# k and v of linear attention fetched as 112 rows and 16 more, in place of 115 and one

## The chip, the cores and the metric

The kernel runs on one core of one Trainium2 chip. The metric is the device time in microseconds; 926.72 us is the median of three runs of the kernel before (926.64 to 927.29). Times inside the kernel are taken from one profiled execution, whose span is 926.5 us. In the profile the engines are PE (TensorE, matrix products), DVE (VectorE), ACT (ScalarE), POOL (GpSimd) and SP (SyncE, which here does nothing but issue transfers). "SPq" is SP's queue: its rows are the times that SP spends on issuing a transfer, not the transfer itself.

## The reference

Linear attention without a softmax, an RMS norm, and a two-layer network with the activation h * erf(softplus(h)):

```python
# q, k, v: (8 batches, 8 heads, 576 positions, 64), float32
kv  = einsum('bhsd,bhse->bhde', k, v)          # 64 x 64 for each head
out = einsum('bhsd,bhde->bhse', q, kv)
out = out / sqrt(mean(out * out, axis=-1) + 1e-6) * g_norm
x   = out.transpose(0, 2, 1, 3).reshape(4608, 512)
h   = x @ w_in                                  # 512 -> 2048
g   = h * erf(softplus(h))
y   = g @ w_out                                 # 2048 -> 512, float32
```

What the change concerns is the first line: kv is a sum over the 576 positions, so it doesn't matter which position lies in which row of which chunk, as long as k and v agree.

## The kernel before

**Stages.** The 4608 tokens are worked in nine token tiles of 512: for each of the eight batches its first 512 positions, and a ninth tile with the last 64 positions of all batches (`x_last`). The network has 16 slices of 128 hidden columns. Tiles 0 and 1 are worked slice by slice in the loop at L822 (step `n` = 0 to 32). Meanwhile `w_in` and `w_out`, which come as 64-bit floats, are turned into float32 (`load_w`, `w_split`, `w_join`, L208 to L263), and from tile 1 on they are cut into three forms [...] and are stored in device memory (`w_upper`, `w_lower`, L645 to L674). From tile 2 on the loop at L976 (step `m`) works four slices at a time: each step reads four `w_in` and four `w_out` pieces of 768 KB back (`load_parts`, L765, issue at L773). A product is a group of eight matmuls into `n_ps` and four into `m_ps` (`product`, L626).

**Attention beside it.** Two heads make a pair, so a batch has four pairs. While tile T is in the network, the four pairs of batch T+1 go through attention, one in each step `m`. `visit` (L428) multiplies q with the kv of the present pair and then forms the kv of the next pair (`kv_products`, L320): five chunks of rows, and for each chunk, each half of its rows and each head one 64-column product at L449, 20 in all. Rows 0 to 63 are the first half, the rest the second. The first pair of batch 1 is done the same way by `prepare` (L353, matmuls at L357). Batch 0 goes another way (`products`, L398): six chunks of 96 rows, fetched in the first microseconds.

**The fetches.** `load_pair` (L123) fetches k and v of one pair. For batches 1 to 7 the 576 positions are cut into five chunks, 576 = 5 * 115 + 1: a first transfer (L141) brings 115 rows of 2 heads x 5 positions x 64 numbers, in which a row holds five successive positions (1280 bytes from one place of device memory), and a second (L146) brings position 575 into row 115 of chunk 0, for both heads. `load_q` (L152) then brings q of the pair in eight pieces (L162), two for each quarter of the partitions, with runs of 32 numbers (128 bytes). `turn` (L314) transposes q in 32 x 32 blocks on DVE (L318) for the visit.

**What sets the order.** The program is written out by hand (`tc.manual_schedule()`, L103): each engine does its instructions in the order of the source. All transfers named here, from the fifth pair on, go out on SP's queue one after another; an issue whose buffer is still in use holds up all behind it. `k_sb`, `v_sb` and `q_sb` have two buffers each (`kvp`), the `w_in` pieces four (`w_in_p`), and the `w_out` pieces seven (`w_out_p`). In the loop at L976 the pieces of weights are asked for at the places given by `FETCH`, one or two at a time, and the pair's loads are part of an attention piece (`loads`, L552):

```python
FETCH = ("", "in", "in", "out", "in", "out", "in", "out out")
places = (0, 2, 3, 5, 6, 8)
```

Of the kernel before, what the change touches and what calls it, by code (L numbers as in the profile page):

```python
# [61 lines left out]
def kernel(  # L62
# [12 lines left out]
    B, H, S, D = q.shape  # L75
# [43 lines left out]
    def chunks(T):  # L119

        return 6 if T == 0 else 5

    def load_pair(i, turned=True):  # L123
        T, p = divmod(i, NP)
        if T >= B:
            return
        pool = early if i in (2, 3) else kvp
        side = nc.scalar if i < 3 else nc.sync
        if T == 0:
            t = pool.tile([P, G if pool is early else S], FP32, name="q_sb", tag="q")  # L130
            t = q_sb[T, p] = t[:, 0:G].rearrange("p (j h d) -> p j h d", j=J, h=2)
            nc.sync.dma_start(
                out=t, in_=q[T, 2 * p : 2 * p + 2, 0:G, :].rearrange("h (p j) d -> p j h d", j=J)
            )
        for name, got, src in (("k", k_sb, k), ("v", v_sb, v)):
            C = chunks(T)
            rows, rest = divmod(S, C)
            assert rest < 2
            t = got[T, p] = pool.tile([rows + rest, 2, C, D], FP32, name=f"{name}_sb", tag=name)
            heads = src[T, 2 * p : 2 * p + 2]  # L140
            side.dma_start(  # L141
                out=t[:rows].rearrange("r h c d -> r h (c d)"),
                in_=heads[:, : S - rest].rearrange("h (r c) d -> r h (c d)", c=C),
            )
            if rest:
                side.dma_start(  # L146
                    out=t[rows:, :, 0], in_=heads[:, S - rest :].rearrange("h r d -> r h d")
                )
        if T > 0 and turned:
            load_q(i)  # L150

    def load_q(i):  # L152


        T, p = divmod(i, NP)
        t = q_sb[T, p] = kvp.tile([P, S], FP32, name="q_sb", tag="q")
        for n in range(P // SQ):
            h, w = divmod(n, D // SQ)
            to = t[n * SQ : n * SQ + SQ].rearrange("a (j b) -> a j b", b=SQ)
            for head, js in ((1 - h, slice(0, G // 2 // SQ)), (h, slice(G // 2 // SQ, S // SQ))):  # L160
                src = q[T, 2 * p + head, :, w * SQ : w * SQ + SQ]
                nc.sync.dma_start(  # L162
                    out=to[:, js], in_=src.rearrange("(j a) b -> a j b", a=SQ)[:, js]
                )
# [12 lines left out]
    for i in range(NP - 1):  # L177
        load_pair(i)
        if i == 0:
            load_last(0)  # L180
            load_last(1)
# [138 lines left out]
    def kv_products(T, p, at, crossed):  # L320


        ks, vs = (x.pop((T, p)) for x in (k_sb, v_sb))
        C = chunks(T)
        for c in range(C):
            for r in range(2):
                rows = (slice(0, D), slice(D, S // C + (c < S % C)))[r]
                for i in range(2):
                    yield partial(
                        nc.tensor.matmul,  # L330
                        at[rows_of[i], 1 - (r ^ i) if crossed else r, kv_cols],
                        lhsT=ks[rows, i, c],
                        rhs=vs[rows, i, c],
                        start=(c == 0),
                        stop=(c == C - 1),
                    )
# [16 lines left out]
    def prepare(T, p):  # L353

        at = at_tile()
        for product_ in kv_products(T, p, at, crossed=False):
            product_()  # L357
        kept.append(partial(kv_kept, T, p, at))
# [7 lines left out]
    def attention(T, p, pools=None, in_parts=False):  # L366
# [15 lines left out]
        def bank(name):  # L382
            if T == B:
                if p == 0:
                    at_pool(2)
                return ps_now[0].tile([P, G], FP32, name=name, tag="at")
            pool, tag = pools.get(name, (ps_at, "at"))
            return pool.tile([P, G], FP32, name=name, tag=tag)

        def square_tile(name):  # L390

            if T == 0:
                return gate.tile([P, G], FP32, name=name, tag="h")
            if apart:
                return attp.tile([P, G], FP32, name=name, tag="sq_lo")
            return qt_tile(name)[:, 0:G]

        def products():  # L398

            kv_ps = st["kv"] = bank("kv_ps")  # L400
            ks, vs, qs = (x.pop((T, p)) for x in (k_sb, v_sb, q_sb))
            C = chunks(T)
            for c in range(C):
                rows = slice(0, S // C + (c < S % C))
                for i in range(2):
                    s = rows_of[i]
                    nc.tensor.matmul(
                        kv_ps[s, s],
                        lhsT=ks[rows, i, c],
                        rhs=vs[rows, i, c],  # L410
                        start=(c == 0),
                        stop=(c == C - 1),
                    )
            if p % 2 == 0:
                nc.tensor.transpose(kv_ps[:, q_tail], q_last[:, p // 2], ident)
            st["qT"] = square_tile("qT")
            for s in rows_of:
                nc.vector.tensor_copy(out=bd[s, s], in_=kv_ps[s, s])
            if p % 2 == 0:
                tails[T] = attp.tile([P, G], FP32, name="qT_last", tag="sq_lo")[:, 0:P]  # L420
                nc.vector.tensor_copy(out=tails[T], in_=kv_ps[:, q_tail])
            st["tail"] = tails[T][:, p % 2 * R : p % 2 * R + R]
            qt_ps = bank("qt_ps")
            for j in range(J):
                nc.tensor.transpose(qt_ps[:, j * P : j * P + P], qs[:, j], ident)
            nc.scalar.copy(st["qT"], qt_ps)

        def visit():  # L428


            qT = ready.pop((T, p))
            at = st["at"] = at_tile()
            x = halves_of(qT[:, 0:G])
            for a, i in ((0, 0), (0, 1), (1, 0), (1, 1)):
                nc.tensor.matmul(  # L435
                    at[rows_of[i if a else 1 - i], a, 0 : 2 * P],
                    lhsT=bd[rows_of[i], (1 - a) * D : (2 - a) * D],
                    rhs=x[rows_of[i], a],
                    start=True,
                    stop=True,  # L440
                )
            for s in rows_of:
                nc.tensor.matmul(
                    at[s, 1, 2 * P : 2 * P + R], lhsT=bd[s, 0:D], rhs=qT[s, G:S], start=True, stop=True
                )
            st["o"] = at[:, :, 0 : 2 * P]
            if then[0] < B:
                for product_ in kv_products(*then, at, crossed=True):
                    product_()  # L449
            if apart:  # L450
                st["sq"] = x_new.tile([P, G], FP32, name="sq", tag="x")
            else:
                st["sq"] = qT[:, 0:G]
            nc.scalar.activation(two(st["sq"]), st["o"], AF.Square)
# [97 lines left out]
        def loads():  # L552
            load_pair(T * NP + p + 2)

        if T == 0:
            return products, apply, halve, mean, norm
# [174 lines left out]
    load_last(2)  # L731
    load_last(3)
    load_pair(NP - 1)

    w_rounds = {
# [86 lines left out]
    for n in range(FIRST * FC + 1):  # L822
        T, f = divmod(n, FC)
# [152 lines left out]
    for m in range(first_batch, batches + 1):  # L976
        T, b = divmod(m, NB)
# [133 lines left out]
```

## Time and profile before

| | before |
|---|---|
| median of three runs | 926.72 us |
| span of the profiled execution | 926.5 us |
| PE busy | 898.8 us |
| PE loading weights | 668.6 us |
| DVE busy | 751.0 us |
| ACT busy | 589.9 us |
| bytes moved | 259.91 MB, mean 281 GB/s |
| transfers k_sb and v_sb, first part | 56 of 287.5 KB |
| transfers k_sb and v_sb, second part | 56 of 0.5 KB |
| transfers of q_sb by L162 | 112 of 40.0 KB and 112 of 32.0 KB |
| transfers of weight pieces | 116 and 112 of 768.0 KB |
| granted TensorE clock | 1.00 throughout |

How to read the views. A group line gives the source line, the engine and the tiles, then counts and times. A wait line reads "engine tile line <- what it waited for: us in total, times, longest". A line of the chain of waits gives the start, the length and the work. A window line gives the stretch in us, its length, the busy time of each engine with the number of instructions in brackets, and at the end the clock, the share in which the core's 16 DMA engines were busy (a mean over the 16, so five busy engines alone show as 5/16 = 0.31) and GB/s. The share can show a little over 1. An engine that is busy all the time can only be made shorter by taking work from it; idle time of another engine costs nothing unless the busy one waits for it.

### The profile page before, as it was taken

The numbers are of one execution on the slowest core, as the hardware profiler recorded it, in microseconds if no ns is written. First come the engines' busy times: TensorE is split into PE (matmuls) and PEld (weight loads), VectorE is DVE, ScalarE is ACT, GpSimd is POOL, SyncE is SP. The second block draws the span as 40 slices with busy tenths as digits, with TensorE's granted clock in tenths as the row PEclk, the third lists the DMA queues.
The fourth block names the chain that finished last, engine by engine and source line by source line (L and its number), as shares of the span: only waits on it lengthen the run. The fifth ranks groups of instructions, "written<-read, shape, count | busy, mean of one in ns | idle before, by whom it ended". The sixth has DMA issues, their size and how long they took to land.

```text
span 926.5 us, 13591 instructions
## 1 busy us (share of the span) xinstructions
PE 898.8 (97%) x4990; PEld 668.6 (72%) x4990; DVE 751.0 (81%) x1088; ACT 589.9 (64%) x783; POOL 2.4 (0%) x10
## 2 busy tenths in 40 slices
PE   6999999988999999999999999999999999999998
PEld 4444445655587888778878888788878888888886
DVE  2799958888588888888888888888888888886777
ACT  3868766767675666656665666666666766665552
POOL 1000000000000000000000000000000000000000
PEclk9999999999999999999999999999999999999999
DMA  9767506698688888988898788887889788778871
GB/s 250 237 190 265 167 1 249 246 378 313 239 287 312 311 312 310 347 308 308 308 337 309 296 310 310 301 306 284 292 313 404 272 286 322 291 288 314 325 271 51
DMA packets 143210, 259.91 MB, mean 281 GB/s; under 512 B 78936, under 2 KB 101800, under 8 KB 143144
## 3 DMA queue, kind: packets, MB, share of 16 engines
q1 hardware_dynamic: 141432, 256.74, 75.7%
q10 hardware_dynamic: 1648, 2.29, 0.9%
q8 instruction: 40, 0.66, 0.3%
q14 instruction: 26, 0.21, 0.1%
q0 software_dynamic: 64, 0.00, 0.0%
HBM read 224.40 MB, written 34.60 MB: 280 GB/s over the span
## 4 chain that ended last, share of the span: by engine, by line
PE 76%; DMA 11%; DVE 6%; ACT 5%; issue 1%; SPq 1%; DVEq 0%; ACTq 0%
PE n_ps L634 41%; PE m_ps L634 20%; PE o_ps L690 6%; PE h_ps L874 4%; DMA w_out_parts<-w_out 4%; DMA w_in_parts<-w_in 2%; DMA w_in<-w_new 2%; DMA v_sb<-in_v_dram 1%; PE at_ps L449 1%; PE at_ps L435 1%; DMA w_raw<-in_moe_w_out_dram 1%; ACT s_sb L911 1%; DMA q_sb<-in_q_dram 1%; DVE h L612 1%; PE at_ps L496 1%
## 5 line engine op out<-in xcount | busy, mean ns | idle before, releaser
L634 PE MATMUL n_ps<-w_out_parts,g_forms 128*128 128x512 f32 x928 | 231.2, 391 | 1.7 <-DMA w_out_parts<-w_out 1.7
L634 PE MATMUL n_ps<-x_forms,w_in_parts 128*128 128x512 f32 x896 | 225.1, 393 | 3.2 <-DMA w_in_parts<-w_in 2.1
L634 PEld LDWEIGHTS n_ps<-w_out_parts,g_forms 128*128 128x128 f32 x928 | 172.4, 188 | 38.4 <-DMA w_out_parts<-w_out 3.3
L634 PEld LDWEIGHTS n_ps<-x_forms,w_in_parts 128*128 128x128 f32 x896 | 166.1, 188 | 41.1 <-ACT h L1024 3.2
L1039 ACT ACTIVATE s<-h 128x512 f32<-128x512 f32 x112 | 71.0, 634 | 180.9 <-DVE h L612 180.9
L612 DVE TENSOR_TENSOR h<-m_ps,h 128x512 f32<-128x512 f32 x116 | 79.9, 689 | 61.5 <-ACT h L1024 39.9
L634 PE MATMUL m_ps<-w_out_parts,g_forms 128*128 128x512 f32 (+1 forms) x468 | 124.3, 388 | 0.0
L634 PE MATMUL m_ps<-x_forms,w_in_parts 128*128 128x512 f32 x448 | 119.8, 389 | 0.0
L690 PE MATMUL o_ps<-w_out_sb,h_sb 128*128 128x512 f32 x224 | 101.5, 596 | 0.2 <-DVE h_sb L820 0.2
L634 PEld LDWEIGHTS m_ps<-w_out_parts,g_forms 128*128 128x128 f32 x468 | 87.5, 188 | 18.4
L634 PEld LDWEIGHTS m_ps<-x_forms,w_in_parts 128*128 128x128 f32 x448 | 84.1, 188 | 17.6
L612 DVE TENSOR_TENSOR e<-m_ps,e 128x512 f32<-128x512 f32 (+1 forms) x117 | 80.3, 687 | 14.1 <-PE m_ps L634 2.9
L1024 ACT ACTIVATE h<-n_ps 128x512 f32<-128x512 f32 x112 | 65.6, 585 | 16.6 <-PE n_ps L634 16.6
L690 PEld LDWEIGHTS o_ps<-w_out_sb,h_sb 128*128 128x128 f32 x224 | 41.3, 189 | 45.3 <-issue 42.8
L578 DVE SCALAR_TENSOR_TENSOR g_forms<-g_forms 128x1024 fp32r<-128x1024 f32 x58 | 71.1, 1225 | 2.0
L575 DVE TENSOR_TENSOR g_forms<-h,g_forms 128x1024 fp32r<-128x1024 f32 x58 | 70.6, 1217 | 1.2 <-ACT g_forms L572 1.1
L572 ACT ACTIVATE g_forms<-h 128x1024 fp32r<-128x1024 f32 x58 | 58.7, 1051 | 14.8 <-PE m_ps L634 10.9
L1071 DVE TENSOR_TENSOR h<-h,s 128x1024 f32<-128x1024 f32 x56 | 65.9, 1218 | 0.0
L874 PE MATMUL h_ps<-xT,w_in_sb 128*128 128x512 f32 x144 | 64.6, 594 | 0.0
L607 DVE SCALAR_TENSOR_TENSOR e<-n_ps,e 128x512 f32<-128x512 f32 x88 | 60.1, 683 | 1.5 <-PE n_ps L634 1.5
L109 ACT ACT_TABLE_LOAD x44 | 56.5, 1283 | 0.8
L874 PEld LDWEIGHTS h_ps<-xT,w_in_sb 128*128 128x128 f32 x144 | 27.1, 190 | 33.4 <-issue 31.6
(119 smaller groups left out, 990.7 us busy)
## 6 DMA issues: line engine op xcount, KB each, us to landing
w_out_parts<-w_out SPq DMA_DIRECT2D x116, 768.0 KB
w_in_parts<-w_in SPq DMA_DIRECT2D x112, 768.0 KB
w_in<-w_new SPq DMA_DIRECT2D x16, 768.0 KB
w_raw<-in_moe_w_in_dram SPq DMA_DIRECT2D x16, 512.0 KB
w_raw<-in_moe_w_out_dram SPq DMA_DIRECT2D x8, 1024.0 KB
out_dram<-e SPq DMA_DIRECT2D x32, 256.0 KB
k_sb<-in_k_dram SPq DMA_DIRECT2D x28, 287.5 KB
v_sb<-in_v_dram SPq DMA_DIRECT2D x28, 287.5 KB
```

The source lines that it names most:

```text
L109: nc.scalar.preload_act_table_set("softplus")
L572: nc.scalar.activation(high, x, AF.Copy, scale=1.0 + 2.0**-13)
L575: nc.vector.tensor_tensor(out=low, in0=x, in1=high.bitcast(FP32), op=ALU.subtract)
L578: nc.vector.scalar_tensor_tensor(out=both, in0=low.bitcast(FP32), scalar=SHIFT, in1=high.bitcast(FP32), op0=ALU.mult, op1=ALU.add,)
L607: nc.vector.scalar_tensor_tensor(out=out_, in0=ps, scalar=scale, in1=out_, op0=ALU.mult, op1=ALU.add)
L612: nc.vector.tensor_tensor(out=out_, in0=ps, in1=out_, op=ALU.add)
L634: nc.tensor.matmul(ps[:, cols], lhsT=weights(form, k), rhs=moving(form, k)[:, cols], start=(form == forms[0] and k == 0), stop=(form == fo ...
L690: nc.tensor.matmul(o_ps[j], lhsT=g[:, j * P : j * P + P], rhs=w_out_sb[:, f, :], start=(f == 0), stop=last,)
L874: nc.tensor.matmul(plain[i], lhsT=w_in_sb[:, i % FC, c], rhs=xT[T][:, c, :], start=(c == 0), stop=(c == KC - 1),)
L1024: nc.scalar.activation(h[:, i], n_ps, AF.Copy, scale=SHIFT - 1.0)
L1039: nc.scalar.activation(s[:, i], h[:, i], AF.Softplus)
L1071: nc.vector.tensor_tensor(out=part(h, half), in0=part(h, half), in1=part(s, half), op=ALU.mult)
```

## The change

The rows of the first transfer are rounded down to a multiple of 16, and what is left goes into the second transfer: 576 = 5 * 112 + 16. A new helper gives the number of rows of a chunk: 128 in chunk 0 and 112 in chunks 1 to 4 (before: 116 and 115). So the first transfer has 112 rows of 1280 bytes per head, and the second 16 rows of 256 bytes per head, into rows 112 to 127 of chunk 0. The second half of the rows in a product is 64 deep for chunk 0 and 48 for the others, in place of 52 and 51. For batch 0 (six chunks of 96) both forms give the same. The purpose is a number of rows that splits evenly over the DMA engines.

```diff
+    def rows_in(T, c):
+
+        rows = S // chunks(T) // 16 * 16
+        return rows + (S - chunks(T) * rows if c == 0 else 0)
+
     def load_pair(i, turned=True):
@@
         for name, got, src in (("k", k_sb, k), ("v", v_sb, v)):
             C = chunks(T)
-            rows, rest = divmod(S, C)
-            assert rest < 2
+            rows, rest = rows_in(T, 1), rows_in(T, 0) - rows_in(T, 1)
             t = got[T, p] = pool.tile([rows + rest, 2, C, D], FP32, name=f"{name}_sb", tag=name)
@@
-                rows = (slice(0, D), slice(D, S // C + (c < S % C)))[r]
+                rows = (slice(0, D), slice(D, rows_in(T, c)))[r]
@@
-                rows = slice(0, S // C + (c < S % C))
+                rows = slice(0, S // C)
```

The last hunk is in `products`, which serves batch 0 only. The lines after the helper are counted by five more in the changed kernel up to `load_pair`, and by four more below it: L141 becomes L145, L146 becomes L150, L162 becomes L166, L773 becomes L777.

## The prediction

> **What bounds the kernel now.** I read the page first (engine shares, slices, transfers), then the matrix engine's waits, the chain of waits, the windows, and the queue of the engine that issues the transfers.
>
> ```profile
> PE 898.8 (97%) x4990; PEld 668.6 (72%) x4990; DVE 751.0 (81%) x1088; ACT 589.9 (64%) x783; POOL 2.4 (0%) x10
> DMA  9767506698688888988898788887889788778871
> k_sb<-in_k_dram SPq DMA_DIRECT2D x28, 287.5 KB
> k_sb<-in_k_dram SPq DMA_DIRECT2D x28, 0.5 KB
> ```
>
> TensorE (PE) is busy 97%: whatever this change does, it can only take from the 926.5 - 898.8 = 27.7 us in which PE stands still. The transfers are 0.8 to 0.9 busy in most slices, a mean over 16 DMA engines. The waits of PE say which of its idle time belongs to transfers:
>
> ```profile
> PE n_ps L634 <- ACT h_sb L889: 3.4, 1, 3.4
> PE n_ps L634 <- ACT h L889: 2.8, 1, 2.8
> PE n_ps L634 <- DMA w_in_parts<-w_in: 2.1, 2, 1.7
> PE at_ps L435 <- DVE qT L318: 2.0, 1, 2.0
> PE n_ps L634 <- DMA w_out_parts<-w_out: 1.7, 2, 0.9
> ```
>
> Four waits for weights make 3.8 us in all. The 2.0 us at L435 ends with a DVE transpose of q, and that DVE instruction had itself waited 3.9 us for a q load. (7.2 us more, at L407, are the first loads of the program, which have 96 rows and don't change.)
>
> The windows show what a 115-row load does to the DMA engines. From 16.5 to 25.6 us four of them are issued (k and v of the two first pairs of batch 1):
>
> ```profile
> 21.00:22.00 1.00, 1.00 (x14) 0.93 (x11) 0.45 (x2) 0.94 (x3) 0.00 (x0) 1.00 0.98 341
> 22.00:23.00 1.00, 0.88 (x2) 0.05 (x1) 0.83 (x2) 1.00 (x3) 0.00 (x0) 1.00 0.36 132
> 24.00:25.00 1.00, 1.00 (x5) 0.60 (x4) 1.00 (x2) 1.00 (x2) 0.00 (x0) 1.00 0.34 124
> 26.00:27.00 1.00, 0.20 (x1) 0.00 (x0) 1.00 (x3) 1.00 (x3) 0.00 (x0) 1.00 0.38 133
> ```
>
> The last two columns are the DMA share and GB/s. A share of 0.34 of 16 is 5.4 engines: about five work, eleven stand idle for 5 us, at 124/5 = 24.8 GB/s each. In saturated windows (573 to 575 us: share 1.03, 420 GB/s) all 16 give 26 GB/s each.
>
> The issuing queue (SP) shows the second effect. Columns are start, length, source line:
>
> ```profile
> 573.13 0.29 SPq L141 DMA_DIRECT2D k_sb<-in_k_dram  x1
> 574.90 1.65 SPq L146 DMA_DIRECT2D k_sb<-in_k_dram  x1
> 576.59 0.42 SPq L141 DMA_DIRECT2D v_sb<-in_v_dram  x1
> 577.36 4.48 SPq L146 DMA_DIRECT2D v_sb<-in_v_dram  x1
> 581.89 7.43 SPq L162 DMA_DIRECT2D q_sb<-in_q_dram  x8
> 589.37 0.46 SPq L773 DMA_DIRECT2D w_out_parts<-w_out  x1
> 590.87 0.75 SPq L773 DMA_DIRECT2D w_in_parts<-w_in  x1
> ```
>
> Issuing two rows and eight small q pieces takes SP 16 us, and behind them four weight loads go out in a burst with nothing to wait for: they were late. SP's own waits name the cause: L162 waited 38.6 us in total on v_sb transfers and 16.7 on k_sb. The burst's fourth load is the one PE then lacks:
>
> ```profile
> 590.87 10.12 DMA w_in_parts<-w_in
> ```
>
> It lands at 601.0 and PE starts at 601.13 after 1.70 us of idleness.
>
> **What the Trainium skill says.** "DMA: Bandwidth & Descriptors", section "Why a DMA increments its semaphore by 16 and not by 1": a load from this queue uses the largest number of engines, up to 16, that divides the slowest dimension of both sides. For 115 that is 5 and for the single row (slowest dimension: 2 heads) 2; for 112 and for 16 it is 16. The trace agrees for 115 (5.4 engines); for 112 nothing here shows it, but 96-row and 128-row loads do reach share 1. Same page, "Queues, rings and completion order": every DMA engine takes the queue's pieces in order, so later loads wait behind the slow five. Same page, "Specifications": pieces under 512 B don't reach line rate; q's pieces of 128 B agree (70 to 150 GB/s at share 0.4 to 0.5 in 583 to 589 us).
>
> **The change part by part.** The instruction orders of PE, DVE, ACT and GpSimd stay as they are, and SP issues the same 651 rows with 112x2x320 in place of 115x2x320 and 16x2x64 in place of 1x2x64.
>
> Matmuls: batches 1 to 7 keep 20 products per pair; the second half of the rows is 64 or 48 deep in place of 52 or 51. In the trace 64-, 52- and 51-row products all take 217 to 218 ns, so 0.
>
> k and v loads: one pair is 2 x (294,400 + 512) = 590 KB. On five engines at 24.8 GB/s each: 4.8 us of those five. On 16 at 420 GB/s: 1.4 us. The five slowest engines get 3.4 us back per pair, 28 times, out of a 23.8 us period, so the five, which by this stand some (4.8 - 1.5)/23.8 x 11/16 = 0.10 above the mean share of 0.83, come down to it.
>
> Small pieces: 32 pieces of 256 B per load in place of 2, so 60 more per pair. q's 2304 pieces of 128 B per pair take about 0.4 x 16 engines x 4.5 us = 29 engine-us, 12.5 ns each; at twice that, 60 x 25 / 16 = 0.1 us spread over all engines. Hidden: PE's work lies over it.
>
> SP time: L141, L146 and L162 together occupy SP (29.9 + 101.3 + 213.5)/26 = 13.3 us per pair after the first 50 us. A 96-row load on 16 engines is issued in 0.33 us, and the quickest eight q loads took 5.8 us: 4 x 0.33 + 5.8 = 7.1 us. So 6.2 us at best. At worst SP still waits for the queue to drain, and only the 3.4 us of backlog is saved. I take 3.4 us: the weight loads behind go out 3.4 us earlier, unless their buffer is still held.
>
> Steady state: the first matmuls of successive attention visits (L435) are 23.81 us apart when nothing is late. The four periods with a DMA wait of PE are 24.80 (378 to 403 us), 25.00 (475 to 500), 25.79 (595 to 621) and 24.66 (669 to 693): 0.99 + 1.19 + 1.98 + 0.85 = 5.0 us over. The recorded idle time is 0.76 + 0.91 + 1.70 + 0.44 = 3.8 us. The longest, 1.98, is below 3.4, so all four should close: between 3.8 and 5.0, I take 4.5. The other periods' excess (25.0 at 281 to 306 us, for instance) ends at ACT h L1024, which a transfer doesn't touch: 0.
>
> Early stage: the w_raw loads at 25.75 us could go at about 22, because the buffer was freed by a DVE join (L263) ending at 20.9. The loads issued at 34.20 and 36.09 us then meet idle engines: 2.1 MB at about 340 GB/s is 6.2 us, so they land near 42.3 in place of 45.88, and the q loads behind them near 45 in place of 47.6 (eight issues of about 0.8 us from 36.5, and 2 us). PE finishes its matmuls before L435 at 46.66: the whole 2.0 us goes. At worst 0; I take 2.0.
>
> Second pass (batch 1, 139 to 257 us): PE stops 3.42 us at 197 and 2.79 us at 227 behind ACT L889. ACT had waited for stores of w_new (1.44 and 1.36 us before the first, 2.15 before the second), and those stores are issued after k, v and q. But the last of those waits ends just as PE ends its own read of the same buffer (190.1; at 220.0 the releaser is PE n_ps), so an earlier store doesn't free it: 0, at most 3.
>
> Start and end: unchanged. Sum: 4.5 + 2.0 = 6.5 us, 926.7 - 6.5 = 920.2.
>
> **The rivals.**
> - Stalls shrink only. All four stalls lie in or after the period in which a batch's results are stored, and there volume counts: 6.29 MB weights + 0.59 + 1.05 stores = 7.9 MB, 18.9 us at 420 GB/s, plus some 5 us in which q runs at low rate: 23.9 of 23.8 us. Spreading k and v can't mend that. Half of 5.0 and half of 2.0: 3.5 us, 923.2. For it: the position of the stalls. Against: eleven idle engines during q.
> - Hidden anyway. The k and v are needed a period later and PE is 97% busy; another load becomes the late one: 926.7. Against: the burst follows SP's delay directly.
> - More than forecast. The stores of w_new also come early enough to shorten the ACT stops: 3 us more, 917.2. Against: PE holds the buffer until the same moment.
> - Slower. The small pieces cost like separate transfers and sit in front of q and weights: 0.1 us a pair on the path, 28 x 0.1 = 2.8, 929.5. For it: 256 B pieces are inefficient. Against: there are 60 beside q's 2304.
>
> **Numbers.** Forecast 0.58; stalls shrink 0.20; more 0.08; hidden 0.09; slower 0.05. Faster: 0.58 + 0.20 + 0.08 = 0.86, same 0.09, slower 0.05. The range goes from 918.0 (full 5.0, 2.0 and some of the ACT stop) to 924.5 (below the 3.5 us case by another 1.3); hidden, slower and the far end of "more" stay out, about 0.19.
>
> **What would show it.** Windows of 22 to 27 us without a share near 0.33; L145/L150 issues on SP near 0.3 to 0.5 us in place of up to 4.95; eight q issues in 6 us or so; no PE wait for w_in_parts, w_out_parts or qT; visits 23.81 us apart between 378 and 693 us. It is wrong if the weights still land late after an early issue (then volume bounds), if SP's L166 still takes 7 to 11 us, or if the time saved at 48 us comes back as a longer ACT stop near 195.

## Result and profile after

The changed kernel took 918.11 us (median of 4 runs, 917.67 to 918.49). The kernel before, run on the same chip, took 927.0 us. The ratio is 0.9898, with a 95% interval from 0.9881 to 0.9916. The profiled spans are 926.5 and 916.5 us, 10.0 us apart, where the prediction had 6.5 (920.2 us, range from 918.0). The direction was right and the gain half as large again. At the ratio, 926.72 us becomes 917.3, just below the range.

The page of the changed kernel first: busy engines, the DMA engines in 40 slices, and the first part of the k load.

```profile
PE 896.7 (98%) x4990; PEld 668.2 (73%) x4990; DVE 749.9 (82%) x1088; ACT 589.6 (64%) x783; POOL 2.4 (0%) x10
DMA  9777507899688998888988889888888688778871
k_sb<-in_k_dram SPq DMA_DIRECT2D x28, 280.0 KB, 9.1
```

PE does the same 4990 matmuls, 2.1 us less busy by the profile. PE's idle time falls from 27.7 to 916.5 - 896.7 = 19.8 us. Where it went is in the waits of PE (three rows that are much the same before and after are left out):

```profile
PE kv_ps L411 <- DMA v_sb<-in_v_dram: 8.4, 4, 6.2
PE at_ps L500 <- DVE bd_kv L345: 1.3, 3, 0.5
PE at_ps L439 <- DVE qT L322: 1.0, 1, 1.0
PE n_ps L638 <- ACT h_sb L893: 1.0, 1, 1.0
PE at_ps L500 <- DVE x_last L461: 0.9, 1, 0.9
PE n_ps L638 <- ACT h L893: 0.5, 1, 0.5
```

Three things are to be seen. No row for w_in_parts or w_out_parts is left (3.8 us before). The two waits for ACT, 3.4 and 2.8 us before, are 1.0 and 0.5; the prediction had left them as they were. And two rows at L500 are new: PE now waits for DVE, 2.2 us in all. The wait for qT, which the prediction saw go, is 1.0 in place of 2.0.

The windows of the first loads of batch 1 (last three columns: clock, DMA share, GB/s):

```profile
22.00:23.00 1.00, 1.00 (x3) 0.30 (x2) 0.96 (x3) 1.00 (x3) 0.00 (x0) 1.00 1.12 269
24.00:25.00 1.00, 1.00 (x3) 0.42 (x3) 0.97 (x3) 0.97 (x2) 0.00 (x0) 1.00 1.17 298
26.00:27.00 1.00, 0.01 (x1) 0.04 (x1) 0.96 (x4) 0.97 (x3) 0.00 (x0) 1.00 1.05 256
```

In place of shares of 0.36, 0.34 and 0.38 at 124 to 133 GB/s all engines work, though at 256 to 298 GB/s and not at the 420 that the prediction took for them. SP's queue in the period that answers to the one shown of before (start, length, line):

```profile
562.96 0.58 SPq L145 DMA_DIRECT2D k_sb<-in_k_dram  x1
563.59 0.68 SPq L150 DMA_DIRECT2D k_sb<-in_k_dram  x1
564.31 0.59 SPq L145 DMA_DIRECT2D v_sb<-in_v_dram  x1
565.78 0.31 SPq L150 DMA_DIRECT2D v_sb<-in_v_dram  x1
567.96 8.88 SPq L166 DMA_DIRECT2D q_sb<-in_q_dram  x8
576.88 0.46 SPq L777 DMA_DIRECT2D w_out_parts<-w_out  x1
```

The rest of the rows, 1.65 and 4.48 us of issue before, takes 0.68 and 0.31. The q load, though, isn't issued any faster (8.88 us here, 7.43 before). Over all 26 pairs after the first 50 us, L141, L146 and L162 took 29.8, 101.3 and 212.6 us (the prediction has 213.5 for the last); L145, L150 and L166 take 26.4, 27.0 and 206.7. That is 3.0 us a pair from the k and v loads and 0.2 from q: 3.2 in all. The mean hides two cases. From 330 us on the k and v loads save 4.4 us a pair and q takes 0.7 more; between 130 and 250 us k and v take 0.3 more, and q saves 2.5. In the whole span SP's waits of L162 for k_sb and v_sb fall from 55.3 us to 8.6, and those for the weight pieces that went out before them rise from 28.9 to 107.6: by the profile, q is issued to a queue that is still full, now of weights.

To place the gain, the span is cut at the first matmul of certain attention visits (L435, L439 after). Each column is the length of a stretch in us: to the first visit; to the sixth; to the ninth (the part of the second pass in which w_new is stored beside k, v and q); to the twelfth; to the last (four whole token tiles); and to the end. "ACT stops" are PE's waits for ACT at L889 (L893, L894), which all lie in the stretch to the ninth visit. "Clock" is what the stretches from the first visit on lost to a granted clock below 1 while PE had work, as (1 - clock) x length. Rows from e1 on are the experiments below.

| kernel | to 1st visit | to 6th | to 9th | ACT stops | to 12th | to last | to end | span | clock |
|---|---|---|---|---|---|---|---|---|---|
| before | 48.65 | 121.03 | 87.65 | 6.2 | 73.05 | 386.83 | 209.29 | 926.5 | 0 |
| after | 47.20 | 121.01 | 82.95 | 1.5 | 72.02 | 382.87 | 210.45 | 916.5 | 0 |
| e1: new rows in batch 1 | 46.41 | 121.34 | 87.73 | 4.6 | 73.75 | 387.45 | 209.32 | 926.0 | 1.7 (to 9th) |
| e2: new rows in next six pairs | 48.02 | 121.02 | 82.79 | 1.3 | 73.46 | 386.65 | 209.46 | 921.4 | 0 |
| e3: new rows in all later pairs | 46.40 | 121.36 | 88.02 | 5.1 | 72.62 | 383.07 | 210.53 | 922.0 | 1.7 (to 9th) |
| e4: before, stores from GpSimd | 46.88 | 121.11 | 87.08 | 3.9 | 74.12 | 384.96 | 209.05 | 923.2 | 1.7 (to 9th) |
| e5: after, stores from GpSimd | 46.38 | 121.36 | 83.80 | 1.8 | 73.11 | 382.86 | 210.29 | 917.8 | 0 |
| e7: 114 rows | 50.17 | 121.04 | 87.94 | 5.1 | 72.70 | 382.83 | 210.52 | 925.2 | 1.7 (to 9th) |
| e8: 115 rows, k and v from GpSimd | 59.61 | 122.48 | 87.13 | 5.4 | 79.67 | 382.90 | 211.21 | 943.0 | 1.7 (to 6th), 3.4 (to 12th) |
| e9: the same, batches 2 to 7 only | 47.92 | 121.03 | 86.64 | 5.0 | 77.74 | 383.48 | 211.09 | 927.9 | 0 |
| e10: after, batches 2 to 7 from GpSimd | 46.47 | 121.27 | 84.13 | 2.4 | 74.30 | 383.13 | 211.0 | 920.3 | 0 |

The gain of the change in this table: 1.45 to the first visit, 4.70 to the ninth, 1.03 to the twelfth, 3.96 to the last, and 1.16 given back after it: 10.0.

### The profile page after: what moved, and what is told of

It is laid out like the page before. It is cut to its first block, busy times and chain, and to the rows that moved or that the text cites. A ratio compares the mean times of both kernels' runs of the same rounds, so it can differ in the third digit from the quotient of the medians.

```text
span 916.5 us, 13591 instructions
## 1 busy us (share of the span) xinstructions
PE 896.7 (98%) x4990; PEld 668.2 (73%) x4990; DVE 749.9 (82%) x1088; ACT 589.6 (64%) x783; POOL 2.4 (0%) x10
## 4 chain that ended last, share of the span: by engine, by line
PE 76%; DVE 10%; DMA 6%; ACT 4%; issue 2%; SPq 1%; DVEq 0%; ACTq 0%
PE n_ps L638 41%; PE m_ps L638 20%; PE o_ps L694 5%; PE h_ps L878 5%; DMA w_in_parts<-w_in 1%; PE at_ps L453 1%; PE at_ps L439 1%; DMA w_in<-w_new 1%; DVE h L616 1%; DMA w_raw<-in_moe_w_in_dram 1%; DMA w_raw<-in_moe_w_out_dram 1%; DVE e L616 1%; DVE g_forms L579 1%; DMA k_sb<-in_k_dram 1%; DMA v_sb<-in_v_dram 1%
```

## Where the unforeseen half came from

The stretch to the ninth visit, with 4.70 us the largest single part, was costed at nothing. Its two PE stops begin with ACT, which writes `w_new` into a buffer whose contents are still on their way to device memory. Three views of the kernel before, in this order: the timeline of ACT (its wait in brackets), SP's queue, and the timeline of PE.

```profile
188.13 0.63 ACT L596 ACTIVATE w_new<-w_out_sb 128x512 fp32r<-128x512 f32 x1 [1.44 <-DMA w_out<-w_new]
190.12 0.63 ACT L596 ACTIVATE w_new<-w_in_sb 128x512 fp32r<-128x512 f32 x1 [1.36 <-DMA w_in<-w_new]
```

```profile
177.41 7.30 SPq L162 DMA_DIRECT2D q_sb<-in_q_dram  x8
184.82 0.39 SPq L672 DMA_DIRECT2D w_out<-w_new  x1
185.32 0.36 SPq L672 DMA_DIRECT2D w_in<-w_new  x1
```

```profile
197.25 0.49 PE L634 MATMUL n_ps<-x_high,w_new 128*128 128x512 f32 x1 [3.42 <-ACT h_sb L889]
```

The same three of the changed kernel:

```profile
184.89 0.62 ACT L600 ACTIVATE w_new<-w_out_sb 128x512 fp32r<-128x512 f32 x1
186.00 0.63 ACT L600 ACTIVATE w_new<-w_in_sb 128x512 fp32r<-128x512 f32 x1 [0.49 <-DMA w_in<-w_new]
```

```profile
176.31 4.22 SPq L166 DMA_DIRECT2D q_sb<-in_q_dram  x8
180.63 0.39 SPq L676 DMA_DIRECT2D w_out<-w_new  x1
181.14 0.36 SPq L676 DMA_DIRECT2D w_in<-w_new  x1
```

```profile
193.35 0.50 PE L638 MATMUL n_ps<-x_high,w_new 128*128 128x512 f32 x1 [0.99 <-ACT h_sb L893]
```

The flight of the w_in store is the same: 185.32 to 190.04 is 4.7 us, 181.14 to 185.92 is 4.8. What differs is when it starts. The numbers it stores were finished by DVE at 179.73 before and at 177.96 after. So the store stood 5.6 us in SP's queue behind k, v and q, and now stands 3.2; here it is q's issue that shrank (7.30 to 4.22 us). That q's pieces had queued behind k and v on the five engines would explain it; no trace shows it directly. ACT's waits fall from 1.44 + 1.36 = 2.80 to 0.49, that is by 2.31, and the PE stop falls by 3.42 - 0.99 = 2.43. At the second stop the store was 5.9 us late (data at 209.38, issue at 215.25) and is 3.7 late (205.24, 208.95). PE there, before and after:

```profile
227.12 0.50 PE L634 MATMUL n_ps<-x_high,w_new 128*128 128x512 f32 x1 [2.79 <-ACT h L889]
220.96 0.50 PE L638 MATMUL n_ps<-x_high,w_new 128*128 128x512 f32 x1 [0.47 <-ACT h L893]
```

The two stops together give 2.43 + 2.32 = 4.75, which is the 4.70 of the table.

The prediction had said that PE holds the same buffer to the same moment. The trace after shows that it doesn't: ACT writes the buffer at 186.00, while PE's m_ps product of that time runs from 187.82 to 188.92. That product reads the next slice's buffer. w_new has four buffers, taken in turn by w_out and w_in, so what ACT writes at 190.12 in the kernel before goes where the w_in slice of 170.00 lay, and PE had multiplied by that one by 184.15. The agreement at 190.1 was a coincidence of two ends.

## The experiments

The kernel before took from 927.5 to 929.7 us (medians) on the chips of the experiments. So each ratio below is against its runs on the same chip. The theory after the result: five DMA engines hold a backlog of k and v; SP's issue stalls behind it; what stands behind that in SP's queue (weight pieces in the steady state, stores of w_new in the second pass) is late by as much. The rivals: (a) the row shape itself matters, not the engines; (b) the lateness comes from the busy engines on whatever queue, so SP's order has no part in it; (c) the early loads bring the gain and carry it through.

### e1, e2, e3: the new rows in one stage alone

The condition is put into the helper. With `i` the number of the pair, e1 has it for batch 1, e2 for the six pairs after it, e3 for the rest (lines are the changed kernel's plus one):

```diff
-    def rows_in(T, c):
+    def rows_in(T, p, c):
 
-        rows = S // chunks(T) // 16 * 16
+        i = T * NP + p
+        rows = S // chunks(T) // 16 * 16 if i < 8 else S // chunks(T)
...
# e2: if 8 <= i < 14
# e3: if i >= 14
```

> 112 + 16 rows only for the four pairs of batch 1 (fetched from 16 to 70 us), 115 + 1 for all other pairs. Theory (three separate gains, as the visits' starting times in the two traces add up): only the early 1.5 us is gained, about 925.3; the PE stops at 197 and 227 us (3.4 and 2.8 us) and the four waits for weights stay. Rival (the gain is one chain: what comes early in the first 50 us shifts everything behind it into a better phase): most of 8.9 us, 920 or less.

> 112 + 16 rows only for pairs 8 to 13 (both first pairs of batch 2 up to the second of batch 3, fetched from 90 to 230 us). Theory (stores of w_new wait on SP's queue behind the 115-row loads, ACT waits for those stores, PE for ACT): PE's two stops fall from 3.4 + 2.8 us to about 1.0 + 0.5, and the time by about 4.7 us, to 922. Rival of the prediction (ACT's last wait is held by PE's own reading of the buffer, so earlier stores free nothing): stops stay at 3.4 and 2.8 us, 926.7.

> 112 + 16 rows only from pair 14 on (fetched from 250 us). Theory (weights issued late behind k, v and q): PE's four waits for w_in_parts and w_out_parts go, some 3.8 us net, about 922.9; the early stop and the stops at 197 and 227 us stay. Rival (volume: the transfers of the periods with stores are too many): the waits stay at half or more, 924.5 or above.

Measured: e1 929.04 us, ratio 1.000 (0.9983 to 1.0016). e2 924.82 us, 0.9948 (0.993 to 0.9966). e3 924.04 us, 0.9946 (0.9927 to 0.9965). The three gains, 0, 0.52 and 0.54%, add up to 1.06%, and the change brings 1.02%; each is uncertain by some 0.18, and within that nothing shows that the parts depend on each other. PE's waits of e2 and e3 (the rows that differ) show which stops each takes.

```profile
PE n_ps L639 <- DMA w_in_parts<-w_in: 4.2, 4, 2.0
PE at_ps L440 <- DVE qT L323: 1.8, 1, 1.8
PE n_ps L639 <- DMA w_out_parts<-w_out: 1.8, 2, 1.1
PE n_ps L639 <- ACT h_sb L894: 0.9, 1, 0.9
PE n_ps L639 <- ACT h L894: 0.4, 1, 0.4
```

```profile
PE n_ps L639 <- ACT h_sb L894: 3.3, 1, 3.3
PE n_ps L639 <- ACT h L894: 1.8, 1, 1.8
PE at_ps L501 <- DVE bd_kv L346: 1.5, 3, 0.6
PE at_ps L501 <- DVE x_last L462: 1.0, 1, 1.0
```

e2 (first fence) keeps all the weight stops and has the two ACT stops at 0.9 and 0.4, as in the full change. e3 (second fence) is the mirror: no weight stop, both ACT stops long. The table says the same: 82.79 us to the ninth visit in e2 alone, 383.07 to the last in e3 alone. (The clock dips of e1 and e3 lengthen their stretch to the ninth visit by 1.7 us. With that taken off, the four profiles with old rows there, before, e1, e3 and e9, need 86.0 to 87.7 us for it and have stops of 4.6 to 6.2; the two with new rows, after and e2, need 83.0 and 82.8 and have 1.5 and 1.3.) Rival (c) falls by the timed runs: e1, with the early loads alone, gains nothing, and e2 and e3 gain without them. (In e1's profile the first visit comes 2.24 us earlier than before and the last 0.53 us earlier; the 1.7 us between are the clock dip, so the profile alone would not decide it.)

e3 also shows the price of the steady gain: the two DVE rows at L501 and 1.2 us more to the end (210.53 against 209.29) come with it, and with nothing else.

On the early stop the profiles don't settle the matter. Of old rows in batch 1, the first visit came at 48.65, 48.02, 46.40, 46.88 and 47.92 us (before, e2, e3, e4, e9); of new rows at 47.20, 46.41, 46.38 and 46.47 (after, e1, e5, e10). e3 has old rows there and no wait for qT, so the 2.0 us of the kernel before isn't owed to five engines alone; the means, 47.6 and 46.6, allow 1 us of effect. e1's timed runs show none, but their interval, 1.5 us to either side, doesn't exclude 1 us.

### e4 and e5: the stores of w_new past SP's queue

GpSimd issues nothing else at that time. If SP's queue alone held the stores up, issuing them there would bring the second-pass gain without any change of rows (e4), and the rest of it to the changed kernel (e5).

```diff
-            nc.sync.dma_start(out=kept, in_=t.bitcast(FP32))
+            nc.gpsimd.dma_start(out=kept, in_=t.bitcast(FP32))
```

> 115 + 1 rows everywhere as before; only the 26 stores of w_new are issued from GpSimd's queue in place of SP's, so they don't stand behind the k, v and q loads. Theory (the store's place on SP's queue is what delays it in the second pass): ACT's waits for w_new stores before 197 and 227 us (1.4 + 1.4 and 2.2 + 1.3) shrink, PE's stops there shrink by 3 us or more in sum, 922 to 924. Rival (the five slow DMA engines delay the stores' data, whatever queue issues them): the stops stay, 926 to 928. A third (issue through GpSimd adds a delay of its own to each store): slower than before.

> The changed kernel, with the 26 stores of w_new issued from GpSimd. In the changed kernel these stores still leave 3 to 4.5 us after DVE has finished their data, behind q's loads on SP. Theory (with k and v spread, nothing slow is left for a store to share an engine with): stores leave at once and land in about 5 us, PE's last stops at 193 and 221 us (1.0 + 0.5) go, 1 to 1.5 us less than the changed kernel. Rival (as with 115 rows, what is gained at issue is lost in the transfer): stores land after 8 to 9 us, no gain or a loss.

Measured: e4 926.63 us, 0.9973 (0.9963 to 0.9984); e5 919.93 us, 0.9897 (0.988 to 0.9914), no better than the change's 0.9898. In e4 the ACT stops are 3.9 us, where the profiles with SP's stores and old rows have 4.6 to 6.2 and the change 1.5, and the gain of 0.27% is half of e2's. (The stretch to the ninth visit shows 0.6 us less; 1.7 us of clock lie over it.) The stores do leave at once, but the chain of waits shows how long one then flies:

```profile
171.80 9.20 DMA w_in<-w_new
```

It is issued at 171.80 and lands 9.2 us later. The same store left at 173.28 in the kernel before and held ACT until 179.77, 6.5 us later; in the changed kernel it flew from 171.52 to 177.98, 6.5 us too. PE's first stop is then another one:

```profile
188.06 0.53 PE L634 MATMUL n_ps<-x_high,w_new 128*128 128x512 f32 x1 [2.18 <-ACT h_sb L889]
196.36 0.50 PE L634 MATMUL n_ps<-x_high,w_new 128*128 128x512 f32 x1 [0.25 <-ACT h_sb L889]
```

The stop that was 3.42 us is 0.25, and a new one stands a slice earlier, behind the long flight. So rival (b) holds in part, by about half if the timed gains of e4 and e2 are compared: out of the queue, the store is late in flight instead. That k and v, issued from 170.0 on and on five engines, are what lengthens the flight is read from the order of the issues; no run shows it apart. The stretch to the last visit is 384.96 us here and 386.83 before, with the same rows and queues in both; that is what two profiles of the same steady code can differ by.

e5 was a miss of the theory that what is left in the second pass (1.46 us of stops) is SP's order. Its stretch to the ninth visit is 83.80 us, not shorter than 82.95: one stop is gone, the other is 1.8 us, and the w_in store of 171.54 takes 7.2 us to land, against 6.5 from SP's queue.

### e6 and e7: 113 and 114 rows

```diff
-        rows = S // chunks(T) // 16 * 16
+        rows = S // chunks(T) if T == 0 else 113
...
# e7: 114
```

The Trainium skill, "DMA: Bandwidth & Descriptors", section "Why a DMA increments its semaphore by 16 and not by 1", says that the largest number up to 16 that divides the slowest dimension is the number of engines: 1 for 113, 6 for 114, 16 for 112. The shape of the rows barely changes. If rival (a) held, e6 would stay near the kernel before.

> 113 + 11 rows in place of 115 + 1, batches 1 to 7. 113 is prime, so by the rule of the largest divisor up to 16 the main transfer uses one engine. Theory (number of engines decides): 578 KB of a pair on one engine at 24.8 GB/s is 23.3 us, beside that engine's share of some 7 MB of weights and stores, 17 us: some 40 us per pair in place of 23.8 in the steady part, 28 pairs by 14 to 16 us, so 1250 to 1400 us. Rival (the number of engines is not what counts; it is the one-row transfer): 918 to 927.

> 114 + 6 rows: six engines for both transfers in place of five and two. Theory (number of engines): k and v of a pair take 3.9 us of six engines in place of 4.8 us of five and 1.4 us when spread, so a quarter to a half of the gain of 112 + 16: 922.5 to 925.5 on a chip where before is 927. Rival (SP's long issue of the one-row transfer on two engines is the cause, 1.3 to 4.95 us each): with six rows it goes and most of the gain comes, 919 or less.

Measured: e6 1407.83 us (one run), half as long again. Two windows and the largest waits of PE in e6:

```profile
24.00:26.00 2.00, 2.00 (x7) 0.79 (x5) 1.83 (x4) 1.94 (x4) 0.00 (x0) 1.00 0.07 25
26.00:28.00 2.00, 0.75 (x3) 0.34 (x3) 1.97 (x4) 1.97 (x4) 0.00 (x0) 1.00 0.07 24
```

```profile
PE at_ps L453 <- DMA v_sb<-in_v_dram: 202.0, 21, 13.3
PE n_ps L638 <- DMA w_in_parts<-w_in: 121.6, 21, 11.2
```

A share of 0.07 is 0.07 x 16 = 1.1 engines, at 24 to 25 GB/s. Two rows less than in the kernel before cost 478 us in this run: it is the engines, not the shape. (Not all of it is waiting: the granted clock was 0.832 in the mean, which is 0.168 x 1406 = 236 us at full clock. It fell to 0.50 after the long stops.) The two waits are the two halves of the mechanism: the load itself comes late, and the weights, which stand behind it in SP's queue and share its engine, come late.

e7 took 923.18 us, 0.9937 (0.9917 to 0.9956). A window of it:

```profile
24.00:25.00 1.00, 1.00 (x8) 0.72 (x7) 0.59 (x3) 0.97 (x3) 0.00 (x0) 1.00 0.40 147
```

0.40 x 16 = 6.4 engines at 147 GB/s: six at 24.5 each. One more engine than before, and yet 0.63 of the 1.02% are there, more than the quarter to half that was expected. The table shows why it isn't in proportion. The steady stretch is 382.83 us, the whole gain; the ACT stops are 5.1 us, within the 4.6 to 6.2 of the profiles with old rows, so of the second pass's gain nothing shows here. (The first visit of this profile is late: PE had waited 2.5 us for batch 0's loads at 12.0 us, and the clock fell to 0.50 from 18.8 to 22.3 us.) The steady stops need the backlog only a little shorter: they were 0.4 to 1.7 us long, and the backlog of a pair falls from 4.8 us to 584 KB / 147 GB/s = 4.0 (an estimate from these rates). SP's issues of k, v and q fall from 13.2 to 11.6 us a pair.

### e8, e9 and e10: k and v from GpSimd

The same skill section says that GpSimd's own descriptor path gives some copies all 16 engines whatever their number of rows. Then 115 rows, issued from there, should lie on all engines: the same shape, another spread.

```diff
-        side = nc.scalar if i < 3 else nc.sync
+        side = nc.scalar if i < 3 else nc.sync if i == 3 else nc.gpsimd
...
# e9, and e10 on the changed kernel
+        side = nc.scalar if i < 3 else nc.sync if i < 8 else nc.gpsimd
```

> 115 + 1 rows as before, but k and v of batches 1 to 7 issued from GpSimd's queue. It separates SP's queue from the DMA engines. If the 115 rows still go to five engines: SP is free of 5 us per pair, q and weights leave earlier but share the five engines, gain 2 to 5 us. If GpSimd's descriptors spread 115 rows over all engines: the whole gain of the change without its layout, 917 to 919. If GpSimd's issue is slow (over 2 us per load and pair) it only delays k and v, which are needed a period later: no loss.

> 115 rows and one, as in the kernel before, but the k and v of batches 2 to 7 are issued from GpSimd; batch 1 stays on SP. Theory (what counts is how many DMA engines a load is spread over, not the shape of the rows): [...] the four stops of PE for weights between 378 and 693 us go, the second pass (139 to 257 us) keeps its stops only as far as batch 1's loads cause them (visits 168 to 255 us: between 83, since the k and v that SP issues ahead of the first stores belong to batch 1 up to about 150 us and to batch 2 after it, and 88). Total 0.5 to 1.0% below the kernel before. Rival (the 115-row shape itself, 575 of 576 rows in odd places, costs, or GpSimd's issue collides with the weights): stops for weights stay or move, total within 0.3% of before or slower.

> The changed kernel with the k and v of batches 2 to 7 issued from GpSimd. Theory: after the change nothing waits for SP's queue in the steady state any more (PE's stops there follow DVE), so moving k and v away from SP frees SP 0.9 us per load and gives nothing: within 0.3% of the change (0.987 to 0.993 of before). Rival: the stores of w_new, which go out on SP behind k, v and q, still leave 3.2 to 4.5 us after their data is ready, so they go out earlier and the two stops of the second pass (0.99 and 0.47 us) close too: 1 to 1.5 us less than the change.

Measured: e8 939.69 us, 1.0111 (1.0081 to 1.0141). e9 930.96 us, 1.0038 (1.0027 to 1.005). e10 922.96 us, 0.9953 (0.9939 to 0.9968). All three are misses in the total. The spread over all engines didn't come either. In e9 between 116 and 121 us, when SP issues nothing and GpSimd has just issued k and v of 115 rows, two windows read

```profile
117.00:118.00 1.00, 1.00 (x4) 0.44 (x3) 0.95 (x3) 0.00 (x0) 1.00 (x2) 1.00 0.29 88
118.00:119.00 1.00, 1.00 (x4) 0.51 (x3) 0.93 (x3) 0.00 (x0) 0.25 (x1) 1.00 0.75 212
```

In the first k is under way alone: 0.29 x 16 = 4.6 engines. In the second k and v are under way together: 12 engines. So a load of 115 rows keeps about five engines from GpSimd's queue too, but k and v lie on different ones. (Counted from the packets of the traces: in e9 never more than 11 of k's and v's are in flight at once, and in e10, with 112 rows, up to 18.) The exception that the skill names for some copies isn't shown by any run here.

And yet the steady stops are gone: from the twelfth visit to the last e8 takes 382.90 us and e9 383.48, as the change does (382.87), with the 115 rows of the kernel before. That closes rival (a) from the other side, and it says more: the steady gain doesn't need 16 engines under each load. What e9 shares with the change is SP's time. k, v and q occupy its queue for 260.6 us after the first 50 us in e9 and for 260.1 in the changed kernel, and for 343.7 in the kernel before. Whether SP's freed time alone does it, or also that k and v no longer share engines, no run separates.

The totals are lost elsewhere. In e8 GpSimd doesn't stand in a queue behind batch 0's loads: it issues k and v of batch 1 from 8.23 us on, beside the first loads, and the first visit comes 11 us later. In e9 the loss is in the stretch to the twelfth visit (77.74 us against 73.05), where the weights are read back for the first token tiles. PE's timeline there, and one step of the chain:

```profile
286.38 2.08 PE L634 MATMUL n_ps<-x_forms,w_in_parts 128*128 128x512 f32 x8 [1.90 <-DMA w_in_parts<-w_in]
293.87 0.72 PE L634 MATMUL n_ps<-w_out_parts,g_forms 128*128 128x512 f32 x2 [3.12 <-DMA w_out_parts<-w_out]
```

```profile
277.78 16.05 DMA w_out_parts<-w_out
```

Without k and v ahead of it, SP comes to q at once, and q's eight pieces then occupy SP for 16.5 us (256.06) and 16.0 us (284.45), where they took 9.7 and 8.6 before. The weights behind them leave no earlier (273.16 and 300.46 us; before 273.48 and 300.43), and one that is issued at 277.78 flies 16 us. That SP's time went from k and v to q is read from the queue. That the loss comes from the competition of two queues for the engines is argued, not shown: no run separates it. e10 has it too, in a smaller form (74.30 us), and ends 5 us behind the change.

## Why the prediction was right and wrong

**The bound, right.** PE stays the bound, and the gain came out of its idle time: of 10.0 us, 7.9 is idle time and 2.1 shorter recorded matmuls, which overlap and whose ends are modelled.

**Spread over engines, right; the rate, too high.** Shares of 1.05 to 1.17 in place of 0.34 to 0.38, as the skill's rule says for 112; e6 and e7 confirm it for 113 and 114 (1.1 and 6.4 engines). The 1.4 us for a pair took 420 GB/s; at the 269 and 298 GB/s of the first two windows 590 KB take 2.0 to 2.2.

**Matmuls and small pieces at nothing, right.** The products of 64 and 48 rows take 218 ns in the median. The 32 pieces per load leave no trace: in the period shown L150 issues in 0.3 to 0.7 us, and the rival "Slower" fell.

**SP time of 3.4 us a pair, right as a mean.** It was chosen as the lower end (3.4 of 6.2), since SP still waits for the queue to drain. It measured 3.0 + 0.2 = 3.2. But the q issues of some 6 us did not come: they take 8.0 us in the mean, which the prediction had named as a sign of being wrong (7 to 11 us). The weights came early enough all the same, since k and v alone give up 4.4 us a pair in the steady part. (SP issues 679 transfers in both traces, not 651.)

**Steady state, 4.5: right in cause, net 3.8.** All four weight stops went, and their periods fell by the full 5.01 to 23.81 us. The periods before 330 us, costed at 0, gave another 1.03. But PE now runs into DVE, as the timeline of PE after shows:

```profile
521.68 0.36 PE L500 MATMUL at_ps<-sq_hi,mean_w 128*128 128x256 f32 x1 [0.52 <-DVE bd_kv L345]
713.43 0.36 PE L500 MATMUL at_ps<-sq_hi,mean_w 128*128 128x256 f32 x1 [0.92 <-DVE x_last L461]
```

Three periods, one in each of three token tiles, are at 24.31, 24.54 and 24.53 us, 1.95 over 23.81 in all, and after the last visit 1.16 us more is spent. From the ninth visit to the end the net is 1.03 + 3.96 - 1.16 = 3.83. The weight stops had hidden this DVE work: it appears in every kernel whose steady stops are gone (e3, e5, e7 to e10) and in none that has them (before, e1, e2, e4).

**Early stage, 2.0: not borne out.** 1.45 in the one pair of traces, nothing in the timed e1, and e3 loses the same stop with the old rows. The w_raw loads did go out earlier (24.00 in place of 25.75 us), but the last load ahead of q, given 6.2 us, took 8.82 (9.79 before). The wait for qT is a near race that a single profile settles either way. I had read a cause out of one trace where a second would have shown scatter.

**Second pass, 0: the step that failed.** "But the last of those waits ends just as PE ends its own read of the same buffer (190.1; at 220.0 the releaser is PE n_ps), so an earlier store doesn't free it." The two ends coincided; the release came from the store. At the second stop the profile itself names PE (first line), but the store of 215.25, with the flight of the first one, would land at 219.97 to 220.04, and in the changed kernel the same instruction waits for the store (second line):

```profile
220.00 0.64 ACT L596 ACTIVATE w_new<-w_in_sb 128x512 fp32r<-128x512 f32 x1 [1.31 <-PE n_ps L634]
213.84 0.63 ACT L600 ACTIVATE w_new<-w_in_sb 128x512 fp32r<-128x512 f32 x1 [1.24 <-DMA w_in<-w_new]
```

It measured 4.70 where 0 was taken and 3 was the bound. The bound was too small as well: it stood for 3 us of 3.42 + 2.79 = 6.2 us of stops, though 1.44 + 1.36 and 2.15 us of ACT waits had been read from the trace. "More than forecast", with 917.2 us, was what happened, and its case against rested on that one misreading. That its total fits so well (917.3 at the ratio) is partly luck: it holds 2.0 us of the early stage that aren't borne out and 3 us where 4.70 came.

The step that would have found it was at hand: the prediction says that SP's queue is 3.4 us shorter per pair and that the stores stand behind q. Subtracting 3.4 from 185.32 puts the store's landing at 186.6 in place of 190.0, and the slice in the buffer told which product had read it last.

## To carry to other kernels

When a transfer is made faster, go through all that stands behind it in its queue, stores too, and for each ask what its landing releases; the stores were half of it here. Where two things end in the same tenth of a microsecond, find out which buffer the instruction writes and who last read that one before taking the nearest end for the cause. Moving a late transfer to another queue brought half of what curing the cause did (e4), and moving the slow loads cured the steady stops but lost more elsewhere (e8, e9). And a removed stop may have hidden another engine: here 3.1 us were given back (1.95 and 1.16), with PE waiting for DVE.

## What was not expected of the hardware

Six engines under each k and v load give the whole steady gain, and about five do too when GpSimd issues the loads; one engine (113 rows) cost 478 us in its run, 236 of them by the clock. A stop of PE can cost more than its length: in e1, e3, e4, e7 and e8 the granted clock falls to 0.50 about the end of a stop (from 1.5 us before it to 0.5 after) and stays there 3.4 us (6.8 once in e8), which costs 1.7 us (3.4). The stops were of 2.2 to 4.0 us, and once, in e7 at 18.7 us, of 1.7. Windows of e1 (its stop of 3.35 us ends at 195.24; the clock is the third figure from the end):

```profile
194.00:195.00 1.00, 0.00 (x0) 0.00 (x0) 0.27 (x1) 0.99 (x3) 0.00 (x0) 1.00 1.03 383
196.00:197.00 1.00, 1.00 (x4) 0.81 (x3) 1.00 (x3) 0.96 (x3) 0.00 (x0) 0.50 0.96 399
```

It doesn't follow each such stop: the kernel before kept 1.00 after 3.42 and 2.79 us, and e9 after 3.12. What decides it isn't shown, nor how often it falls in the timed runs.

Single engines gave 24 to 25 GB/s in three cases (25 for one, 147 for six, 124 for five), but with 112 rows all 16 together gave 269 to 298, which is 17 to 19 each. k and v of 115 rows kept about five engines each from either queue, but from GpSimd's on different ones, so that both together had 12 (212 GB/s); its issue takes 1.17 us for each, where SP's took 0.33 to 0.42 in the first loads of batch 1. And SP's q issue stretches when k and v leave the queue ahead of it (16.0 and 16.5 us for eight pieces in place of 8.6 and 9.7): in these two pairs the time at which the weights get their turn stayed the same, whatever stood before them.
